# A list in place of a planner for the filler work between the last block's score steps

## The chip, the cores and the metric

The kernel runs on one core of one Trainium2 chip. The metric is the device time of one execution in microseconds (us), as the median of several runs. One execution was also taken by the hardware profiler; every duration below comes from that profile.

## What is computed

The input x has 2048 rows of 448 values (bfloat16). Its rows are normalised, and three terms are added:

```
xn  = layernorm(x)
A   = softmax(mask(q k^T / sqrt(28))) v @ wo      # 16 heads of 28; row i sees rows i-255 .. i
B   = (gelu(xn @ w_gate) * (xn @ w_up)) @ w_down  # inner width 1792
out = x + A + B
```

## The kernel before

**Tiling.** The rows are cut into four blocks of 512 (`NB` = 4, `QB` = 512). The inner width of 1792 is 14 slices of 128 (`NF` = 14); slices p and p+7 form a pair, since one weight load of 64 rows holds half of the inputs for each, so that the two matmuls of a pair run beside each other in the two halves of the array (`chunk`, L418; the matmul is L426). A pair takes seven chunks, 14 matmuls. The output of a block is four tiles of 128 rows; each tile (`gen_down`, L382) sums 4 matmuls with `wo` (L392, the attention's output `oN`) and 14 with `wd` (L397, the feed-forward's product `hT`) in one bank of PSUM, adds x on the vector engine (L402) and sends the rows out.

**Stages of a block.** Attention (L547) comes first, in ten steps. Each step has a group of score matmuls into the tile `sc` (L626), then one exponential of 128x2048 on ScalarE (L632), then three multiplications by masks on the vector engine (L534), which are queued only in the next step. `sc` takes four of the eight PSUM banks and there is one of it, so the scores of a step cannot start before the exponential of the step before is over. Three steps (4, 6 and 9, the dictionary `pvs`) begin with a PV product, which multiplies finished probabilities by v (L587) into two banks `ov`; the fourth product comes in the next stage. After a PV product ScalarE copies one half (L571) and the vector engine adds the other (L572). The sums of the softmax come from two 32x32 transposes on the vector engine (`sums` L559, `inverse` L567) with a reciprocal between (L560), and GpSimd scales the result into `oN` (`scale_o`, L553). The two transposes write the same single buffer (`l`), which the scaling reads.

Then comes the gated stage (`gated`, L448): for each of the seven pairs p a gate product into `gt` (L426), its gelu on ScalarE (L467), and a multiplication by the up product. Pairs in `early` have their up product already, copied to `hT` in SBUF by the vector engine (`gen_up`, L433, the copies are L444; the multiplication is L472). For other pairs the up product is made in this stage (`up`, L453), stays in PSUM as `u`, and is multiplied from there (L475). After each pair a hook does the next of `sums` and `inverse` with `scale_o` (`after`, L669).

**What sets the order.** The whole program is recorded in the order in which the Python code issues it; each engine runs its own instructions in that order and waits on semaphores. Filler matmuls are put between the score steps by generators, wrapped in a `Feed` (L34). `Feed.run` issues matmuls up to the next `yield`, which tells their planned nanoseconds; a negative number marks the end of a unit, and HOLD keeps a feed from going on within a step. The planner `share` (L55) runs feeds until a step's planned share is used up. In blocks 0 to 2 the fillers are the products for the next block, and from block 1 on the down tiles of the block before. In the last block, `feeds[0]` is the down work of block 2 (4 tiles, 72 matmuls) and a second feed makes up pairs ahead, five of them (L797), in steps that a dictionary `plan` names (L799). After the last gated stage the four down tiles of block 3 stand alone (L843 to L845); its last tile is cut in two halves.

**Banks.** The four PSUM banks beside `sc` are handed out first in, first out by `take` (L250) and returned by `give` (L261): a down tile takes one, an up pair two, a PV product two. `give` is called when the reading instruction is recorded, so the next user of the bank waits for that instruction on the chip.

Of the kernel before, what the change touches and what calls it, by code (L numbers as in the profile page):

```python
# [15 lines left out]
S, D, H, Dh, F = 2048, 448, 16, 28, 1792  # L16
P = 128
NT = S // P
NF = F // P
# [5 lines left out]
HOLD = True  # L25
# [29 lines left out]
def share(feeds, first, second):  # L55

    want = [first, second]
    while True:
        can = [i for i, f in enumerate(feeds) if f.gens and want[i] > 190 and not f.held]
        if not can:  # L60
            return
        i = max(can, key=lambda i: (not feeds[i].closed, want[i]))
        for f in feeds:
            if f is not feeds[i]:
                f.closed = False
        want[i] -= feeds[i].run()
# [9 lines left out]
def kernel(  # L76
# [305 lines left out]
    def gen_down(qb):  # L382

        hT, oN = hTs[qb], oNs[qb]
        for tt in range(4):
            t = 4 * qb + tt
            cs = slice(tt * P, (tt + 1) * P)
            for lo, up in ((0, D),) if t < NT - 1 else ((0, D // 2), (D // 2, D)):
                w = up - lo
                po = take("po")  # L390
                for g in range(4):
                    nc.tensor.matmul(po[:, 0:w], lhsT=oN[:, g, cs], rhs=wo[:, g, lo:up], start=(g == 0), stop=False,  # L392
                                     skip_group_check=True)
                    if g % 2:
                        yield 380 * w // D
                for f in range(NF):
                    nc.tensor.matmul(po[:, 0:w], lhsT=hT[:, f, cs], rhs=wd[:, f, lo:up], start=False, stop=(f == NF - 1),  # L397
                                     skip_group_check=True)
                    if f % 2 and f < NF - 1:
                        yield 375 * w // D  # L400
                res = work.tile([P, D], bf16, name="res", bufs=2)
                nc.vector.tensor_tensor(out=res[:, 0:w], in0=po[:, 0:w], in1=x_sb[:, t, lo:up], op=ALU.add)  # L402
                give(po)
                nc.sync.dma_start(out=outv[:, t, lo:up], in_=res[:, 0:w])
                last_res[:] = [res]
                yield 375 * w // D

    def new_hT(qb):
        hT = blk.tile([P, NF, QB], bf16, name="hT", tag="hT")
# [23 lines left out]
    def gen_up(qb, ps):  # L433

        for p in ps:
            us = [take("ue") for _ in range(2)]
            for c in range(7):
                chunk(us, wu, p, qb, c)
                if c == 2:
                    yield 640  # L440
                if c == 5:
                    yield 640, HOLD
            for i in range(2):
                nc.vector.tensor_copy(out=hTs[qb][:, p + 7 * i, :], in_=us[i])  # L444
            give(*us)
            yield -320

    def gated(qb, early, last_v, flush, hook):  # L448

# [97 lines left out]
    def attention(qb, feeds, aux, plan):  # L547
# [55 lines left out]
        for i, (scores, ncol, edges) in enumerate(steps):  # L603
            while (qb, scores[-1][0]) not in done:
                feeds[0].run()
            for fd in feeds:
                if fd.held:
                    fd.run()
            if i in pvs:
                pv(pvs[i])  # L610
            while fresh:
                apply_masks(*fresh.pop(0))
            if not qb and i - 1 in pvs:
                sums()
                inverse()
            if qb and i - 1 in pvs:
                sums()
            if qb and i - 2 in pvs:
                inverse()
            ss = phase[0].pool.tile([P, 4, QB], f32, name="sc", tag="s")  # L620
            p_sb = work.tile([P, 4, QB], bf16, name="p_sb", bufs=5)
            for g, half, kt, q0, nq, col in scores:
                k0, nk = (64 * half, 64) if half is not None else (0, P)
                for j in range(4):
                    r = slice(32 * j, 32 * j + Dh)
                    nc.tensor.matmul(ss[k0:k0 + nk, j, col:col + nq], lhsT=kT[r, g, kt * P + k0:kt * P + k0 + nk],  # L626
                                     rhs=qT[r, g, qb * QB + q0:qb * QB + q0 + nq], start=True, stop=True,
                                     tile_position=(32 * j, k0), skip_group_check=True)
                parts.setdefault(g, []).append((half, kt, q0, nq, col, p_sb))
            if not qb and i == 2:  # L630
                rstd(6, 2)
            nc.scalar.activation(out=p_sb[:, :, 0:ncol], in_=ss[:, :, 0:ncol], func=ACT.Exp, scale=SCALE)  # L632
            flush()
            if qb:
                fresh.append((p_sb, edges))
            else:
                for m in edges:
                    masked(p_sb, *m)
            while later:
                scale_o(*later.pop(0))  # L640
            left = len(steps) - i
            if left == 1:
                drain(feeds)
            elif not qb:
                share(feeds + [Feed()], 1e12, 0)
            else:
                to = plan.get(i, 0)
                whole = sum(f.left for f in feeds) + STEP * left + PV * sum(j > i for j in pvs)
                ahead = STEP + PV * (i + 1 in pvs) + (360 if to > 1000 else 0)
                late = 400 if i == 0 else 0  # L650
                want = (whole - late) / (left + 0.2) + late - ahead - to
                if i in pvs:
                    had = feeds[0].left
                    share(feeds[:1], min(1100, want), 0)
                    want -= had - feeds[0].left
                if qb == NB - 1:
                    share(feeds[:1], want, 0)
                    share(feeds, 0, to)
                else:
                    share(feeds, want, to)  # L660
            if aux:
                aux.pop(0)()

# [108 lines left out]
    for qb in range(NB):  # L772
        if qb in (1, 3):
            tc.mark_branch_hint_location("general", hint="LikelyTaken",
                                         engines=[mybir.EngineType.DVE if qb == 1 else mybir.EngineType.PE])
        early = ()
        aux, plan = [], {}
        if qb < 2:
            if qb:
                aux = [lambda: rstd(12, 4)]  # L780
            else:
                aux = [ahead, ahead2, ahead3, lambda: fill_pads(False), lambda: fill_pads(True), lambda: None,
                       lambda: stat(8), lambda: stat(9), lambda: stat(10), lambda: stat(11), lambda: rstd(8, 4)]
        if qb == 0:
            new_hT(0)
            early = (1, 2, 3)
            feeds = [Feed((gen_qk(0, (1, 2, 3), [(t, pvs[t]) for t in (2, 3)]), 3 * QK1 + 360),
                          (gen_up(0, (1,)), UP1), (gen_v(1, (4,)), 1500), (gen_up(0, (2,)), UP1), (gen_v(1, (6,)), 1500),
                          (gen_up(0, (3,)), UP1), (gen_qk(1, range(4)), PROJ - 3000))]
        else:  # L790
            feeds = [Feed((gen_down(qb - 1), DOWN))]
            if qb < 3:
                feeds.append(Feed((gen_proj(qb + 1), PROJ)))
                plan = {0: 1140, 1: 1140, 2: 1300, 4: 1300, 6: 1300, 7: 870}
            else:
                new_hT(3)
                early = (1, 2, 3, 4, 5)  # L797
                feeds.append(Feed((gen_up(3, early), UP1 * len(early))))
                plan = {1: 1280, 2: 1280, 4: 1280, 6: 1280, 7: 1280}  # L799
        if qb:  # L800
            swap(qb, nc.sync)
        score_pool(1)
        rest, after, flush = attention(qb, feeds, aux, plan)
        nc.scalar.preload_act_table(ACT.Gelu_apprx_tanh)
        score_pool(2)
        if qb not in hTs:
            new_hT(qb)

        def hook(f):
            after(f)  # L810
            if qb < 3 and f == 4:
                collect(qb + 1)
            if qb < 3 and f == 10:
                deliver(qb + 1)
            if f >= 4 and qb < 2:
                t = 4 * qb + 4 + f // 2
                if f < 12:
                    norm(t + 2)
                    dma_transp(t + 2)
                    if qb == 0:  # L820
                        stat(t + 6)

        gated(qb, early, rest, flush, hook)
        if qb < NB - 1:
            nc.scalar.preload_act_table_set("natural_log_exp_and_others")
# [142 lines left out]
```

## Time and profile before

| what | us |
|---|---|
| median of 3 runs | 219.06 (218.66 to 219.39) |
| the profiled execution's own time | 219.12 |
| its span in the trace | 217.40 |
| its time outside the span | 1.72 |
| TensorE (PE) busy in the span | 212.0 |
| vector engine (DVE) busy | 151.9 |
| ScalarE (ACT) busy | 132.8 |
| GpSimd (POOL) busy | 46.9 |
| block 3, first score matmul | starts at 157.02 |
| block 3, gated stage, first up pair | starts at 185.39 |
| last down tiles, first matmul | starts at 199.87 |

An instruction's row tells its start, its duration, its engine, the line of the code, and what it writes and reads. Matmuls overlap in their pipeline: a matmul of 448 columns shows 352 ns, but the next starts 189 ns after it. What a matmul costs the engine is therefore the distance from its start to the next one's start, not its duration. On the vector engine, too, the next instruction starts about 80 ns before the end of the one ahead where it does not depend on it.

### The profile page before, as it was taken

Reading aid. Unit: us, or ns where it says so; the run is one execution under the profiler, and the core shown is the slowest. Engines: PE = TensorE matmul, PEld = TensorE weight load, DVE = VectorE, ACT = ScalarE, POOL = GpSimd, SP = SyncE. Lnnn points to the kernel's source line nnn. Section 1 sums busy time; section 2 is a strip of 40 time slices with the busy share of each in tenths; the row PEclk is TensorE's granted clock in tenths of the full one; section 3 lists DMA queues with packets and bytes.
Section 4 is the critical chain, followed back from the end, with each engine's and each line's share of the span. In section 5 each row is a group of like instructions: output and inputs, shape, how many; then the busy total and the mean of one; then the engine's idle time right before and its main releaser. Section 6 shows DMA issues by size and latency. Waiting matters only on the chain.

```text
span 217.4 us, 6061 instructions
## 1 busy us (share of the span) xinstructions
PE 212.0 (97%) x2581; PEld 97.5 (45%) x2581; DVE 151.9 (70%) x346; ACT 132.8 (61%) x129; POOL 46.9 (22%) x80
## 2 busy tenths in 40 slices
PE   7999999999999999999999999999999999999993
PEld 2433343444444454444444544444444445444562
DVE  7787898599666883588566795477347799479521
ACT  4588779672978776613778788423576776565000
POOL 5277987320000130022000022022000022022001
PEclk9999999999999999999999999999999999999999
DMA  6993599933510000102320000200030000000011
GB/s 192 273 227 52 125 237 227 281 123 72 79 41 24 24 23 27 22 0 53 81 64 21 24 3 21 59 11 0 0 78 18 5 24 24 24 2 0 26 33 38
DMA packets 23232, 14.45 MB, mean 66 GB/s; under 512 B 9792, under 2 KB 23200, under 8 KB 23200
## 3 DMA queue, kind: packets, MB, share of 16 engines
q1 hardware_dynamic: 22256, 13.73, 26.9%
q8 instruction: 21, 0.34, 0.7%
q10 hardware_dynamic: 944, 0.29, 0.6%
q14 instruction: 11, 0.09, 0.2%
HBM read 8.69 MB, written 2.18 MB: 50 GB/s over the span
## 4 chain that ended last, share of the span: by engine, by line
PE 96%; ACT 1%; DVE 1%; issue 1%; DVEq 0%
PE po L397 21%; PE gt L426 20%; PE u L426 14%; PE sc L626 6%; PE po L392 6%; PE ue L426 6%; PE ov L587 5%; PE pq L237 4%; PE pv L237 4%; PE pk L237 3%; PE wps L196 2%; PE pq L243 1%; PE pv L243 1%; PE s L237 1%; ACT p_sb L632 0%
## 5 line engine op out<-in xcount | busy, mean ns | idle before, releaser
L632 ACT ACTIVATE p_sb<-sc 128x2048 bf16<-128x2048 f32 (+2 forms) x42 | 73.8, 1757 | 12.7 <-PE sc L626 9.4
L467 ACT ACTIVATE ge<-gt 128x1024 bf16<-128x1024 f32 x28 | 28.7, 1024 | 39.6 <-PE gt L426 39.0
L397 PE MATMUL po<-wd,hT 128*128 128x448 bf16 (+1 forms) x238 | 49.0, 342 | 0.0
L553 POOL TENSOR_TENSOR oN<-oc,l 128x512 bf16<-128x512 f32 x12 | 16.0, 1333 | 136.3 <-DVE l L567 85.3
L426 PE MATMUL gt<-xnT,wg 64*128 64x512 bf16 x224 | 45.3, 376 | 0.0
L426 PE MATMUL gt<-xsw,wg 64*128 64x512 bf16 x168 | 40.7, 376 | 0.0
L475 DVE TENSOR_TENSOR hT<-ge,u 128x512 bf16<-128x512 bf16 x40 | 25.8, 679 | 18.3 <-PE u L426 9.8
L426 PE MATMUL u<-xnT,wu 64*128 64x512 bf16 x160 | 33.2, 376 | 0.0
L397 PEld LDWEIGHTS <-hT 128*128 128x128 bf16 x238 | 21.4, 98 | 18.7 <-issue 2.8
L426 PEld LDWEIGHTS <-wu 64*128 64x128 bf16 x392 | 18.8, 94 | 23.8 <-issue 3.8
L426 PE MATMUL u<-xsw,wu 64*128 64x512 bf16 x120 | 29.1, 376 | 0.0
L426 PEld LDWEIGHTS <-wg 64*128 64x128 bf16 x392 | 18.8, 94 | 22.7 <-issue 0.3
L534 DVE TENSOR_TENSOR p_sb<-p_sb,masks 128x256 bf16<-128x256 bf16 (+1 forms) x90 | 26.8, 352 | 1.8 <-ACT p_sb L632 1.8
L626 PE MATMUL sc<-qT,kT 28*64 28x320 bf16 (+7 forms) x640 | 16.9, 263 | 0.2
L402 DVE TENSOR_TENSOR res<-po,x_sb 128x448 bf16<-128x448 f32 (+1 forms) x17 | 10.0, 589 | 8.8 <-PE po L397 8.6
L392 PE MATMUL po<-wo,oN 128*128 128x448 bf16 (+1 forms) x68 | 15.6, 343 | 0.0
L572 DVE TENSOR_TENSOR oc<-oc,ov 128x512 f32<-128x512 f32 x12 | 8.2, 686 | 10.6 <-ACT oc L571 10.6
L544 POOL TENSOR_SCALAR_AFFINE_SELECT p_sb<-p_sb 128x512 bf16<-128x512 bf16 (+1 forms) x20 | 14.2, 730 | 3.7 <-ACT p_sb L632 3.5
L426 PE MATMUL ue<-xnT,wu 64*128 64x512 bf16 x64 | 13.6, 377 | 0.0
L626 PEld LDWEIGHTS <-kT 28*64 28x64 bf16 (+1 forms) x640 | 7.8, 102 | 11.5 <-issue 9.9
L444 DVE CAST hT<-ue 128x512 bf16<-128x512 f32 x16 | 10.2, 678 | 3.8 <-PE ue L426 3.7
L559 DVE STREAM_TRANSPOSE l<-oc 128x512 f32<-128x512 f32 x16 | 11.2, 703 | 1.6 <-POOL oN L553 1.6
(89 smaller groups left out, 232.8 us busy)
## 6 DMA issues: line engine op xcount, KB each, us to landing
out_dram<-res SPq DMA_DIRECT2D x15, 112.0 KB
xsw<-xnT SPq DMA_DIRECT2D x8, 192.0 KB
x_sb<-in_A_x_dram SPq DMA_DIRECT2D x3, 448.0 KB
wu<-in_B_w_up_dram SPq DMA_DIRECT2D x4, 336.0 KB
wd<-in_B_w_down_dram SPq DMA_DIRECT2D x3, 448.0 KB
wg<-in_B_w_gate_dram SPq DMA_DIRECT2D x2, 448.0 KB
wg<-in_B_w_gate_dram SPq DMA_DIRECT2D x2, 336.0 KB
wraw<-in_A_wqkv_dram SPq DMA_DIRECT2D x2, 252.0 KB
```

Of the source, the lines that this page charges most:

```text
L237: nc.tensor.matmul(ps, lhsT=lhs(c), rhs=rhs(c), start=start and c == 0, stop=stop and c == 2, skip_group_check=True)
L392: nc.tensor.matmul(po[:, 0:w], lhsT=oN[:, g, cs], rhs=wo[:, g, lo:up], start=(g == 0), stop=False, skip_group_check=True)
L397: nc.tensor.matmul(po[:, 0:w], lhsT=hT[:, f, cs], rhs=wd[:, f, lo:up], start=False, stop=(f == NF - 1), skip_group_check=True)
L426: nc.tensor.matmul(ps, lhsT=w[r, c, p * P:(p + 1) * P], rhs=x, start=c == 0, stop=c == 6, tile_position=(64 * hi, 0), skip_group_check=True)
L467: nc.scalar.activation(out=ges[p][:, :, :], in_=gt[:, :, :], func=ACT.Gelu_apprx_tanh)
L475: nc.vector.tensor_tensor(out=hT[:, p + 7 * i, :], in0=ge[:, i, :], in1=u, op=ALU.mult)
L534: nc.vector.tensor_tensor(out=reg, in0=reg, in1=m, op=ALU.mult)
L544: nc.gpsimd.affine_select(out=reg, in_=reg, pattern=mid + [[1 if diag else -1, min(w, P)]], compare_op=ALU.is_ge, fill=0.0, base=0 if diag ...
L553: nc.gpsimd.tensor_tensor(out=oN[:, g, :], in0=oc[:, :], in1=inv, op=ALU.mult)
L559: nc.vector.transpose(out=l1[:, :, :].rearrange("p a b -> p (a b)"), in_=oc[:, :])
L626: nc.tensor.matmul(ss[k0:k0 + nk, j, col:col + nq], lhsT=kT[r, g, kt * P + k0:kt * P + k0 + nk], rhs=qT[r, g, qb * QB + q0:qb * QB + q0 + ...
L632: nc.scalar.activation(out=p_sb[:, :, 0:ncol], in_=ss[:, :, 0:ncol], func=ACT.Exp, scale=SCALE)
```

## The change

Four things change in the code.

1. `gen_down` yields after every matmul instead of every second one, and takes the 14 slices of `hT` in another order, with 6 and 13 last.
2. `gen_up` yields after each chunk; HOLD stays for block 0 alone.
3. In the last block, a list tells for each of the ten steps how many yields of the down feed `d` and of the up feed `u` are run, in place of the planner and `plan`. One yield of `d` is one matmul, one yield of `u` is a chunk, two matmuls that run beside each other.
4. `early` in the last block has six pairs, 1 to 6, not five.

```diff
     def gen_down(qb):
+        order = [f for f in range(NF) if f % 7 < 6] + [6, 13]
...
-                    if g % 2:
-                        yield 380 * w // D
-                for f in range(NF):
-                    nc.tensor.matmul(po[:, 0:w], lhsT=hT[:, f, cs], rhs=wd[:, f, lo:up], start=False, stop=(f == NF - 1),
+                    yield 187 * w // D
+                for n, f in enumerate(order):
+                    nc.tensor.matmul(po[:, 0:w], lhsT=hT[:, f, cs], rhs=wd[:, f, lo:up], start=False, stop=(n == NF - 1),
                                      skip_group_check=True)
-                    if f % 2 and f < NF - 1:
-                        yield 375 * w // D
+                    if n < NF - 1:
+                        yield 187 * w // D
...
-                yield 375 * w // D
+                yield 187 * w // D
...
     def gen_up(qb, ps):
                 chunk(us, wu, p, qb, c)
-                if c == 2:
-                    yield 640
-                if c == 5:
-                    yield 640, HOLD
+                if c < 6:
+                    yield (213, HOLD) if qb == 0 and c == 5 else 213
...
-            yield -320
+            yield 330
...
     def attention(qb, feeds, aux, plan):
             left = len(steps) - i
-            if left == 1:
+            if isinstance(plan, list):
+                for feed, n in plan[i]:
+                    for _ in range(n):
+                        feed.run()
+            elif left == 1:
                 drain(feeds)
...
-                if qb == NB - 1:
-                    share(feeds[:1], want, 0)
-                    share(feeds, 0, to)
-                else:
-                    share(feeds, want, to)
+                share(feeds, want, to)
...
                 new_hT(3)
-                early = (1, 2, 3, 4, 5)
-                feeds.append(Feed((gen_up(3, early), UP1 * len(early))))
-                plan = {1: 1280, 2: 1280, 4: 1280, 6: 1280, 7: 1280}
+                early = (1, 2, 3, 4, 5, 6)
+                d, u = feeds[0], Feed((gen_up(3, early), UP1 * len(early)))
+                feeds.append(u)
+                plan = [[(d, 11)], [(d, 7), (u, 3)], [(u, 11)], [(u, 7)], [(d, 18)], [(u, 7)], [(d, 13)], [(d, 5), (u, 6)],
+                        [(u, 8)], [(d, 18)]]
```

## The prediction, made before the changed kernel ran

> **What bounds the kernel now.** I read the page's first part, then its chain that ended last, then the same chain in order of time for block 3, then the timeline of the places that the change touches.
>
> ```profile
> PE 212.0 (97%) x2581; PEld 97.5 (45%) x2581; DVE 151.9 (70%) x346; ACT 132.8 (61%) x129; POOL 46.9 (22%) x80
> ...
> PE 96%; ACT 1%; DVE 1%; issue 1%; DVEq 0%
> ```
>
> The matrix engine is on the chain for 96% of the span. But a busy PE may hide a wait, so I compared distances from start to start. The chain in order of time (start, length, what) has them:
>
> ```profile
> 152.56 1.51 PE u L426 x14
> ...
> 161.42 1.62 PE ue L426 x14
> 163.04 0.35 PE sc L626 x16
> ...
> 185.46 1.62 PE u L426 x14
> 187.07 1.51 PE gt L426 x14
> ```
>
> The reader is to see two lengths for the same 14 matmuls: 1.51 when another up or gate product follows, 1.62 where a stretch is entered from, or left for, another shape (up is 64 rows deep, down 128, scores 32). In unrounded starts a matmul of 448 columns is followed after 189 ns by its like and after 282 to 285 by an up, PV or score matmul; an up pair after 213 by its like and after 306 by scores. **A switch of shape costs 93 to 96 ns.** From 157.02 to the end, each distance is its usual value or that plus a switch: before, the engine waits for nothing in block 3. Hence time can be won only by fewer switches, and is lost by every wait that the new order opens.
>
> **1. Fewer switches: -0.28 us.** Listed in issue order, block 3's score phase had 5 switches down to up, 5 up to scores, 3 down to PV, 1 down to scores: 14. Afterwards it has 2 down to up, 3 up to scores, 3 up to PV, 3 down to scores: 11. Leaving the scores costs the same whatever follows (block 0: 211 ns into up, 210 and 211 into q, behind the same 256 columns). The step from the last gate to the down tiles stays one switch. So 3 x 0.095 = 0.28. The sixth pair is 14 matmuls moved from the end of the gated stage into the score phase: no matmul is added. Its two vector multiplications from PSUM (680 ns each, L475) become two copies (680, L444) and one multiplication (650, L472).
>
> **2. Step 0 becomes too short: +0.37 us.** The table load delays its exponential:
>
> ```profile
> 156.71 1.28 ACT L825 ACT_TABLE_LOAD   x1
> ...
> 157.02 0.42 PE L626 MATMUL sc<-qT,kT 28*64 28x320 bf16 x16
> ...
> 158.01 1.88 ACT L632 ACTIVATE p_sb<-sc 128x2048 bf16<-128x2048 f32 x1
> ...
> 160.13 0.43 PE L626 MATMUL sc<-qT,kT 28*64 28x320 bf16 x24
> ```
>
> The exponential ends at 159.88; 14 down matmuls covered that, and the next scores started at 160.13. The list puts 11 there: 3 x 0.189 = 0.57 less, so PE is ready at 159.56. In block 0, where scores do wait, they start 0.05 behind the exponential (14.96 to 15.01): here 159.94. The wait is 0.37.
>
> The other steps: scores need 0.50 to 0.73 until the exponential starts, 1.88, and 0.05. Step 1 has 0.36 (scores) + 1.42 (7 down and a switch) + 0.74 (3 chunks and a switch) = 2.52 against 0.55 + 1.88 + 0.05 = 2.48. Steps 3 and 5 have 0.36 + 1.59 + 0.68 (PV) = 2.63 against 2.48. The rest are longer: 2.8 to 3.9. No wait, with 0.04 to spare in step 1.
>
> **3. The PV product of step 9 comes before its banks are free: +0.9 us.** Two up pairs now lie close together ahead of it (the sixth chunk of pair 5 in step 7, then pair 5's end and pair 6 in step 8), and the PV product takes pair 5's two banks, which the vector engine must first copy out (L444). That engine's queue ahead of these copies is, from the scores of step 6 on (call their start 0; in the profile 173.94): the addition of PV, masks of step 5, `inverse` of group 0, masks of step 6, `sums` of group 1, an output addition, masks of step 7, `inverse` of group 1.
>
> ```profile
> 176.15 0.70 DVE L567 STREAM_TRANSPOSE l<-inv_all 128x512 f32<-128x512 f32 x1
> ...
> 176.89 1.29 DVE L444 CAST hT<-ue 128x512 bf16<-128x512 f32 x2
> 177.02 1.27 POOL L553 TENSOR_TENSOR oN<-oc,l 128x512 bf16<-128x512 f32 x1 [25.64 <-PE ue L426]
> ...
> 182.46 1.27 POOL L553 TENSOR_TENSOR oN<-oc,l 128x512 bf16<-128x512 f32 x1 [4.17 <-DVE l L567]
> ...
> 182.81 1.60 DVE L534 TENSOR_TENSOR p_sb<-p_sb,masks 128x256 bf16<-128x256 bf16 x3
> ```
>
> Up to `inverse` the order is the old one, so it ends at 176.85, or 2.91. GpSimd's scaling, which started 0.17 behind it here and 0.08 behind it at the three later groups, then runs to 4.26 or 4.35. Before, two copies from PSUM filled that time, unharmed (1.29). Now the masks of step 6 stand there. Three masks take 0.82 alone, but 1.60 where they met a scaling (last pair of rows): they end some 0.6 behind it. With the usual overlap `sums` starts at about 4.65; it could not before the scaling's end in any case, since it overwrites `l`. Then by rows: `sums` 0.91, output addition 0.56, masks 0.74, `inverse` 0.62 to the next start: the first copy starts at 7.48 and ends at 8.17, the second at 8.77. PE's way: step 6 is 0.36 + 2.55 (13 down and a switch) = 2.91; step 7 0.36 + 1.04 (5 down) + 1.37 (6 chunks) = 2.77; step 8's 0.36 + 1.80 (8 chunks) brings it to 7.84. The first half of PV waits until 8.2, the second, which starts 0.003 behind it when nothing waits, until 8.8; of the 0.68 for PV only some 0.1 is done by then. **Wait: about 0.9.** Without the collision it is 0.6. If instead the mask starts first and holds GpSimd back, `sums` comes later and it is 1.1.
>
> The Trainium skill ("SBUF — State Buffer", section "Who interferes with whom") says that a vector operation with two SBUF inputs and a GpSimd operation that reads SBUF exclude each other, and that issue order decides who blocks. The trace agrees on the exclusion (1.60 against 0.82). By that rule the second mask, due at 3.03 by this reckoning, would go first if the scaling starts at 3.08, and the whole sum would be 0.2 higher. I keep GpSimd first, since three of four rows put its start 0.08 behind `inverse`, at 2.99.
>
> **4. The last down tiles reach `oN` too early: +0.47 us.** The sixth pair's 1.51 were the cover for GpSimd's last scaling:
>
> ```profile
> 197.67 1.62 POOL L553 TENSOR_TENSOR oN<-oc,l 128x512 bf16<-128x512 f32 x1 [2.27 <-DVE l L567]
> ...
> 199.87 0.93 PE L392 MATMUL po<-wo,oN 128*128 128x448 bf16 x4
> ```
>
> The scaling of group 3 ends at 199.29. It hangs on ScalarE's first gelu by a chain (transposes, multiplications, two scalings of 1.62) which the change leaves as it is; so it still ends 12.38 behind the start of the first gate product (186.91). PE now needs 1.60 for that gate, 0.67 for PV, 9.08 for the six other gates, 0.10 for the switch, and reaches the fourth `wo` matmul, which reads group 3, 0.57 later: at 12.02. Add 0.1 to 12.38 for signal and weight load: a wait of 0.47 (0.35 to 0.6). The new order of slices does its part: pair 6's product is ready some 1.4 before its matmul, and nothing else is late.
>
> **5. Finer yields in blocks 1 and 2: nothing.** In issue order, a few steps there give one down matmul (0.19) to a neighbour. The shortened steps had 0.40 and 0.56 between exponential and scores, and need 0.05. Down next to v products is no switch (189).
>
> **Sum.** -0.28 + 0.37 + 0.9 + 0.47 = +1.46 on the profiled execution's 219.12: 220.6. The median is 219.06, 0.06 lower, which is nothing here. Measurement can tell about 0.3%, 0.66 us, from no change.
>
> **The rivals.**
>
> - *As forecast*, within 219.9 to 221.0: 0.66.
> - *More waits*: steps 1, 3 and 5 have 0.04 to 0.15 to spare; a copy that delays a bank, or a recut step in blocks 1 and 2, adds 0.1 at each, +0.4 in all: 221.0 and somewhat over. Against it, step 1 alone is really close. 0.12.
> - *Only one of parts 3 and 4 binds.* PV's copies keep up, because the vector engine has idle times of 0.7 to 1.0 in this phase before: -0.28 + 0.37 + 0.47 = +0.56, 219.7. Against: those idle times lay where it waited for up products, and in steps 6 to 8 the list leaves none. 0.11.
> - *Not slower*: the vector engine's queue and the scalings run early enough for both PV and the down tiles. Then -0.28 + 0.37 = +0.09: 219.2. It decides from 0.9 us of the 5.8 us queue in part 3, and 0.47 in part 4. For it, pairs 3 and 4 are copied earlier than before; against it, each duration is a row. 0.07.
> - *Faster*: the scores at 160.13, 173.94, 176.78 and 182.27 each start 0.22 to 0.25 behind an exponential. If that were a wait in disguise, longer steps would free 4 x 0.2 = 0.8, and with half of parts 3 and 4 gone the time would be 218.3. Against: the distances there equal those of steps with 0.4 to spare, and block 0 restarts at 0.05. 0.04.
>
> That the list does not do what it says is excluded by the order of the built instructions: it gives 72 down yields and 42 chunks, as needed.
>
> **The numbers.** Likeliest 220.6. The range 219.6 to 221.3 leaves out the last two cases and tails of the others. Slower by over 0.3% (above 219.7): forecast, more waits and a part of the third, 0.82. Within: 0.14. Faster: 0.04.
>
> **What would show it.** In the changed profile: scores of step 1 at 0.05 behind the end of the first exponential; 0.9 lost between up and PV ahead of step 9's scores, behind copies L444; a scaling on GpSimd that masks of step 6 run into; 0.4 to 0.5 inside the first four `wo` matmuls, ended by L553. The forecast falls if PV starts right behind the up pair in step 9.

## The result and the profile after

| what | us |
|---|---|
| before, median of 6 runs | 218.99 (218.57 to 219.39) |
| changed, median of 6 runs | 220.13 (219.84 to 220.53) |
| changed over before | 1.0052 (1.0039 to 1.0064) |
| profiled execution of the changed kernel, its own time and its span | 220.07 and 218.2 |

The changed kernel is slower by half a per cent. The spans of the two profiled executions (217.4 and 218.2) differ by 0.8, which is less than what block 3 lost, since the changed kernel's execution happened to start block 1 earlier by 0.38 (54.87 against 55.24; see the last section). From block 1's first score to block 3's first score both take 101.78. I therefore compare one distance, from **block 3's first score to the last matmul**: 56.43 before, 57.63 after, **+1.20**. It is used for all runs below.

The page's part on the chain, of the changed kernel, answers to the 96% of before:

```profile
PE 84%; DVE 8%; ACT 3%; issue 2%; POOL 1%; DVEq 0%; ACTq 0%
```

PE is no longer nearly the whole chain. At a wait the chain passes to the engine waited for and follows that one back for as long as it is busy, so the missing 12% are not lost time: the waits, read below, add up to 1.52 us, 0.7% of the span. The waits of the changed kernel in block 3 and behind name them (engine and line, what it waited for: total us, times, longest):

```profile
PEld L393 <- POOL oN L551: 0.7, 1, 0.7
...
PE sc L624 <- ACT p_sb L630: 0.3, 1, 0.3
PE ov L585 <- DVE hT L442: 0.3, 1, 0.3
PE po L393 <- POOL oN L551: 0.2, 1, 0.2
```

Before, this list had no PE row. The idle times here count from the modelled end of a matmul, so they understate what was lost; distances from start to start give it. Line numbers are those of each run's own file: in the changed kernel `wo` is L393, and what comes after `gen_up` has moved up by two lines.

**Step 0.** The timeline of the changed kernel, from step 0's scores to step 1's:

```profile
156.65 0.42 PE L624 MATMUL sc<-qT,kT 28*64 28x320 bf16 x16
...
157.63 1.88 ACT L630 ACTIVATE p_sb<-sc 128x2048 bf16<-128x2048 f32 x1
157.77 1.49 PE L397 MATMUL po<-wd,hT 128*128 128x448 bf16 x7
...
159.56 0.43 PE L624 MATMUL sc<-qT,kT 28*64 28x320 bf16 x24 [0.31 <-ACT p_sb L630]
```

The exponential ends at 159.51 and the scores start 0.05 later. The distance from the last down matmul to the scores is 658 ns where a switch makes it 283: **0.375 lost**.

**Steps 6 to 9.** The vector engine's queue, GpSimd and the PV product, from the same timeline:

```profile
176.31 0.70 DVE L565 STREAM_TRANSPOSE l<-inv_all 128x512 f32<-128x512 f32 x1
176.94 1.86 DVE L532 TENSOR_TENSOR p_sb<-p_sb,masks 128x256 bf16<-128x256 bf16 x3
...
177.19 1.46 POOL L551 TENSOR_TENSOR oN<-oc,l 128x512 bf16<-128x512 f32 x1 [26.18 <-DVE l L565]
...
178.73 0.70 DVE L557 STREAM_TRANSPOSE l<-oc 128x512 f32<-128x512 f32 x1
...
181.47 2.44 DVE L442 CAST hT<-ue 128x512 bf16<-128x512 f32 x4
...
182.17 0.32 PE L585 MATMUL ov<-p_sb,v_sb 64*32 64x320 bf16 x4
182.77 0.73 PE L585 MATMUL ov<-p_sb,v_sb 64*32 64x320 bf16 x44 [0.28 <-DVE hT L442]
```

The three masks of step 6 take 1.86 instead of 0.82, since the third is locked out until GpSimd's scaling is over at 178.65: it alone shows 1.36 instead of 0.28, and ends 0.15 behind the scaling. The copies of pair 5 then start at 181.47, and PV begins in two parts, each some 0.05 behind the end of one copy (182.12 and 182.72). Distances of 455 instead of 306, and 587 instead of 3: **0.73 lost**.

**The last tiles.**

```profile
199.59 1.62 POOL L551 TENSOR_TENSOR oN<-oc,l 128x512 bf16<-128x512 f32 x1 [2.27 <-DVE l L565]
...
200.27 0.74 PE L393 MATMUL po<-wo,oN 128*128 128x448 bf16 x3
...
201.27 0.36 PE L393 MATMUL po<-wo,oN 128*128 128x448 bf16 x1 [0.25 <-POOL oN L551]
```

Three `wo` matmuls run, and the fourth waits for the scaling of group 3, which ends at 201.21: a distance of 603 instead of 189, **0.41 lost**.

The three add to 1.52; the distance grew by 1.20; so 0.32 was won elsewhere. Three switches fewer were expected to give 0.28; where the other 0.04 comes from is told with the last experiment.

### The profile page after: what moved, and what is told of

Same layout as the page of the kernel before. It is cut to its first block, busy times and chain, and to the rows that moved or that the text cites. A ratio compares the mean times of both kernels' runs of the same rounds, so it can differ in the third digit from the quotient of the medians.

```text
span 218.2 us, 6052 instructions
## 1 busy us (share of the span) xinstructions
PE 211.5 (97%) x2572; PEld 97.9 (45%) x2581; DVE 151.8 (70%) x347; ACT 132.8 (61%) x129; POOL 47.1 (22%) x80
## 4 chain that ended last, share of the span: by engine, by line
PE 84%; DVE 8%; ACT 3%; issue 2%; POOL 1%; DVEq 0%; ACTq 0%
PE po L397 18%; PE gt L426 15%; PE u L426 13%; PE sc L624 5%; PE po L393 5%; PE ue L426 5%; PE pv L237 4%; PE pq L237 4%; PE ov L585 4%; PE pk L237 3%; PE wps L196 2%; DVE p_sb L532 2%; POOL oN L551 1%; PE pq L243 1%; ACT p_sb L630 1%
## 5 line engine op out<-in xcount | busy, mean ns | idle before, releaser
L473 DVE TENSOR_TENSOR hT<-ge,u 128x512 bf16<-128x512 bf16 x38 | 24.5, 679 | 18.4 <-PE u L426 9.6
L426 PE MATMUL u<-xnT,wu 64*128 64x512 bf16 x152 | 31.5, 376 | 0.0
L397 PEld LDWEIGHTS <-hT 128*128 128x128 bf16 x238 | 22.4, 98 | 19.0 <-issue 1.8
L426 PE MATMUL u<-xsw,wu 64*128 64x512 bf16 x114 | 27.6, 376 | 0.0
L393 PE MATMUL po<-wo,oN 128*128 128x448 bf16 (+1 forms) x68 | 16.2, 343 | 0.2 <-POOL oN L551 0.2
L426 PE MATMUL ue<-xnT,wu 64*128 64x512 bf16 x72 | 15.3, 377 | 0.0
L426 PE MATMUL ue<-xsw,wu 64*128 64x512 bf16 x54 | 13.2, 377 | 0.0
L442 DVE CAST hT<-ue 128x512 bf16<-128x512 f32 x18 | 11.4, 676 | 2.1 <-PE ue L426 2.1
```

Of the source, the lines that this page charges most:

```text
L426: nc.tensor.matmul(ps, lhsT=w[r, c, p * P:(p + 1) * P], rhs=x, start=c == 0, stop=c == 6, tile_position=(64 * hi, 0), skip_group_check=True)
L473: nc.vector.tensor_tensor(out=hT[:, p + 7 * i, :], in0=ge[:, i, :], in1=u, op=ALU.mult)
```

## The experiments

Each run was timed in five rounds beside the kernel before. "Distance" is from block 3's first score to the last matmul.

| run | distance | time, median | over before (95% interval) |
|---|---|---|---|
| before | 56.43 | 218.99 to 219.06 | |
| changed | 57.63 | 220.13 | 1.0052 (1.0039 to 1.0064) |
| e1_step0 | 57.28 | 219.58 | 1.0035 (1.0024 to 1.0046) |
| e2_wo_late | 57.21 | 219.90 | 1.0040 (1.0025 to 1.0055) |
| e2b_wo_after12 | 57.80 | 220.40 | 1.0064 (1.0046 to 1.0082) |
| e3_chunk | 57.26 | 219.67 | 1.0035 (1.0023 to 1.0046) |
| e9_no_scaling | 57.03 | 219.61 | 1.0028 (1.0013 to 1.0042) |
| e5_yields_only | 56.82 | 219.65 | 1.0023 (1.0011 to 1.0035) |
| e4_three | 56.48 | 219.18 | 1.0001 (0.9988 to 1.0013) |
| e7_copies_first | 56.13 | 218.81 | 0.9988 (0.9974 to 1.0002) |
| e8_switches | 56.98 | 219.61 | 1.0028 (1.0015 to 1.0041) |

Against the kernel before, the medians move as the distances do, within 0.3 us. The intervals of the five runs with a single edit of the changed kernel (e1 to e3 and e9) all overlap that of the changed kernel, so by time alone they can hardly be told from it: what they show is read from their traces, one execution each.

### Step 0: e1_step0

```diff
-                plan = [[(d, 11)], [(d, 7), (u, 3)], [(u, 11)], ...
+                plan = [[(d, 13)], [(d, 5), (u, 5)], [(u, 9)], ...
```

> The changed kernel with the first three entries of the list recut: 13 down in step 0, 5 down and 5 chunks in step 1, 9 chunks in step 2. Theory (the exponential of step 0, held up by the table load, is what step 1's scores wait for): that wait of 0.38 us goes, steps 1 and 2 are then 2.56 and 2.37 us long against 2.48 and 2.42 needed, so 0.05 comes back: 0.3 less than the changed kernel, some 219.8 us, with the waits at step 9's PV and at the fourth wo matmul as they were. Rival (time lost in step 0 is only moved, since the first steps have too little work in all): 0.1 or more waits again in front of the scores of steps 2 or 3, and the time stays at 220.1.

Measured: the wait is gone, 57.28, 0.36 less; 0.02 is left ahead of step 3's scores (a distance of 326 instead of 306). The waits at PV and at the fourth `wo` are as before (454 and 589, 600). The timeline of this run has no wait in front of step 1's scores:

```profile
157.41 1.88 ACT L630 ACTIVATE p_sb<-sc 128x2048 bf16<-128x2048 f32 x1
157.55 1.86 PE L397 MATMUL po<-wd,hT 128*128 128x448 bf16 x9
...
159.34 0.43 PE L624 MATMUL sc<-qT,kT 28*64 28x320 bf16 x24
```

So the first steps had enough work in all; it was in the wrong ones.

### The last tiles: e2_wo_late and e2b_wo_after12

```diff
-                for g in range(4):
-                    nc.tensor.matmul(... oN[:, g, cs] ... start=(g == 0) ...)
-                for n, f in enumerate(order):
-                    nc.tensor.matmul(... hT[:, f, cs] ... stop=(n == NF - 1) ...)
+                heads = [(oN, wo, g) for g in range(4)]
+                ffs = [(hT, wd, f) for f in order]
+                seq = heads + ffs if qb < NB - 1 or tt else FIRST
```

`FIRST` is the order of the first tile of block 3: the ten slices of pairs 0 to 4, `heads`, then slices 5, 12, 6 and 13 in the first run; `ffs[:12] + heads + ffs[12:]` in the second.

> The changed kernel, where the first down tile of block 3 takes its matmuls in another order: ten slices of hT (pairs 0 to 4), then the four with wo, then the slices of pairs 5 and 6. Theory (the wait of 0.41 us in the last tiles is for GpSimd's scaling of group 3): the wait goes, since the fourth wo comes 1.9 us later; 219.7 us. Rival (the vector engine's products for pairs 5 and 6 are just as late, and oN only hides them): a wait of 0.4 us stays, at one of the last four matmuls of that tile, and the time stays at 220.1.

> As the run with late wo, but twelve slices (pairs 0 to 5) come before wo. In the changed kernel's trace the product of pair 5 is locked out by GpSimd's scaling and ends 0.5 us behind it, and its matmul would now stand sixth, 0.95 us behind the tile's start. Theory (scaling and lock together set what is ready when): the wait is not removed but grows to about 0.6, in front of the sixth matmul, behind the vector engine's L470; 220.3 us. Rival (only oN is late): no wait, 219.7 us.

Measured: with ten slices ahead the wait is gone and the distance falls by 0.42. With twelve ahead it is 0.17 longer than in the changed kernel: the sixth matmul comes 778 ns behind the fifth, a wait of 0.59. The timeline of that run shows why:

```profile
199.78 1.62 POOL L550 TENSOR_TENSOR oN<-oc,l 128x512 bf16<-128x512 f32 x1 [2.27 <-DVE l L564]
200.23 2.32 DVE L469 TENSOR_TENSOR hT<-ge,hT 128x1024 bf16<-128x1024 bf16 x2
...
200.46 1.12 PE L396 MATMUL po<-wd,hT 128*128 128x448 bf16 x5
...
202.01 1.31 PE L396 MATMUL po<-wd,hT 128*128 128x448 bf16 x6 [0.42 <-DVE hT L469]
```

Five matmuls run; the sixth reads the product of pair 5, which was locked out by the scaling until 201.40 and ended 0.55 later. Both `oN` and that product are late because of the same scaling; the order of ten, four, four steps around both.

### PV of step 9: e3_chunk and e9_no_scaling

```diff
-                [(d, 5), (u, 6)], [(u, 8)], [(d, 18)]]
+                [(d, 5), (u, 7)], [(u, 7)], [(d, 18)]]
```

> The changed kernel with one chunk moved from step 8 to step 7, so that pair 5 ends in step 7 (5 down, 7 chunks; then 7 chunks). Its copies out of PSUM are then queued ahead of step 7's masks and of the transpose of group 1. Theory (step 9's PV product waits for pair 5's two banks): the wait of 0.74 us in front of and inside PV goes. The copies of pair 6 are still queued behind masks and transpose, and step 9's down tile takes one of its banks, so 0.35 to 0.5 comes back in front of that tile's first wo: 0.25 to 0.4 less than the changed kernel, 219.8 us. Rival (PV waits for the masks of step 7 on its probabilities): those masks come 1.2 us later than before, and the wait in front of PV grows; 220.5 us or more.

Measured: 0.38 less. The wait around PV is gone, and one of 0.36 (499 instead of 137) has come in front of the first `wo` of step 9's down tile:

```profile
181.75 0.82 DVE L532 TENSOR_TENSOR p_sb<-p_sb,masks 128x256 bf16<-128x256 bf16 x3
...
182.41 0.75 PE L585 MATMUL ov<-p_sb,v_sb 64*32 64x320 bf16 x48
...
183.11 1.25 DVE L442 CAST hT<-ue 128x512 bf16<-128x512 f32 x2
...
183.81 0.92 PE L393 MATMUL po<-wo,oN 128*128 128x448 bf16 x4 [0.29 <-DVE hT L442]
```

The masks of step 7 now end 0.16 behind PV's start, and PV does not wait: it was the banks, not the probabilities. The second run takes GpSimd's scaling out of this place:

```diff
         def scale_o(g, oc, inv):
+            if qb == NB - 1 and g == 0:
+                nc.scalar.copy(out=oN[:, g, :], in_=oc[:, :])
+                return
```

> The changed kernel, but in the last block group 0 is not scaled on GpSimd: ScalarE copies it unscaled (so the output leaves out the softmax's division for heads 0 to 3 of block 3). Nothing else is moved. Theory (step 9's PV wait of 0.74 us exists because GpSimd's scaling and the masks of step 6 lock each other out, 1.86 us for masks that take 0.82 alone): the vector engine's queue is 1.0 us earlier, and the wait falls to 0.15 or less: 57.63 - 0.6 = 57.0 us from block 3's first score to the last matmul, 219.5 us. Rival (the list simply gives the vector engine too much in steps 6 to 8, with or without the lock): 0.5 or more of the wait stays, 57.4 us, 220.0.

Measured: 57.03, 0.60 less, as the theory had it. The masks of step 6 take 0.79, and `sums` (L560) follows at once:

```profile
176.88 0.79 DVE L532 TENSOR_TENSOR p_sb<-p_sb,masks 128x256 bf16<-128x256 bf16 x3
...
177.59 0.71 DVE L560 STREAM_TRANSPOSE l<-oc 128x512 f32<-128x512 f32 x1
...
181.97 0.88 PE L588 MATMUL ov<-p_sb,v_sb 64*32 64x320 bf16 x48
```

`sums` starts 1.33 behind the start of step 6's transpose, where it was 2.41. The masks of step 7 then wait for their exponential, so the copies are 0.6 earlier, and of the 0.73 at PV 0.14 is left, between its halves. So four fifths of that wait come from the scaling, and the rest from the queue as it is. That the lock, by which scaling and masks exclude each other, is the cause, as the theory says, is not shown: without the scaling, `sums` need not wait for the buffer `l` either, and in the changed kernel scaling and third mask ended within 0.15 of each other. An estimate from rows says that the buffer alone would do most of it. Without the lock the scaling would take 1.27 and end at 177.19 + 1.27 = 178.46, and in the kernel before a transpose that waited for `l` started 0.04 behind a scaling (195.43 behind 195.39): `sums` would start at 178.50, 0.23 earlier than it did, of the 1.08 by which it is late. A second buffer `l` was not tried.

### The finer yields alone: e5_yields_only

The kernel before with the changed `gen_down`, and nothing else.

> The kernel before, with gen_down alone as changed (a yield after each matmul, slices 6 and 13 last); planner, plan and five early pairs as before. Theory for blocks 1 and 2 (moving single down matmuls between steps costs nothing): block 3's first score starts as far behind block 1's first score as before, 101.78 us. In the last block the planner cuts other steps: it leaves the last down matmul of a tile to step 2, right ahead of an up pair that takes this tile's bank, whose output addition is queued behind the masks: a wait of about 0.4 there, 219.4 us. Rival (the yields do nothing anywhere): 219.0 us and no wait.

Measured: 101.78 from block 1's to block 3's first score, and a wait of 0.41 in front of the second half of an up pair in step 2 (417 instead of some 3):

```profile
162.89 1.29 DVE L444 CAST hT<-ue 128x512 bf16<-128x512 f32 x2 [2.14 <-PE ue L426]
...
163.81 0.39 PE L426 MATMUL ue<-xnT,wu 64*128 64x512 bf16 x1
...
164.23 0.39 PE L426 MATMUL ue<-xsw,wu 64*128 64x512 bf16 x2
...
164.83 0.61 DVE L402 TENSOR_TENSOR res<-po,x_sb 128x448 bf16<-128x448 f32 x1
```

The size is as expected, but the cause is another. The wait ends 0.05 behind the second copy of the up pair before (163.50 to 164.18), and the output addition, which the expectation blamed, starts only 0.60 after the wait is over. Since the tile now ends in step 2, its bank is returned behind both banks of that pair, and the queue of banks hands the new pair those two. In the kernel before, the tile's bank came first, and the new pair took it and the pair's first. In blocks 1 and 2 the yields cost nothing; in the last block they would have cost 0.4 under the planner. The list ends its tile in step 1, and the changed kernel shows no such wait.

### Together: e4_three, e7_copies_first, e8_switches

> The three single edits that removed a wait, together (first three list entries recut, late wo in the first down tile of block 3, one chunk from step 8 to step 7). Theory (the waits are independent, since PE waits for nothing between them): from the changed kernel's 57.63 us between block 3's first score and the last matmul, 0.36, 0.42 and 0.38 go as in the single runs: 56.47; the wait of 0.5 at step 9's first wo stays. Time as before, 219.0. Rival (each removed wait is partly given back to the next): 56.7 or more, 219.3.

Measured: 56.48, as the sum of the single gains has it. The waits are independent. One remains, 0.36 at step 9's first `wo`. The next run moves the vector engine's transpose, in step 8, behind the copies:

```diff
-            if qb and i - 2 in pvs:
+            if qb and i - 2 in pvs and not (isinstance(plan, list) and i == 8):
                 inverse()
...
                 for feed, n in plan[i]:
                     for _ in range(n):
                         feed.run()
+                if i == 8:
+                    inverse()
+                    scale_o(*later.pop(0))
```

> The three edits together, and in step 8 of the last block the transpose of group 1 and its scaling are issued behind the copies of pair 6 instead of ahead of pair 5's. Theory (that transpose, 0.63 us, is what makes pair 6's copies late for step 9's down tile): the wait of 0.5 goes, no wait over 0.05 is left in block 3, and what remains against the kernel before are three switches of shape fewer: 56.43 - 0.28 + 0.05 = 56.2 us from block 3's first score to the last matmul, 218.8 us, 0.1% under the kernel before. Rival (the scaling, now later, is in some other way late): a wait in front of PV of group 3 or of the last tiles, and 56.5 or more.

Measured: 56.13, 0.30 under the kernel before, with no wait over 0.02. By time it is 218.81 and the ratio 0.9988, with an interval that just reaches 1: a gain that the trace shows and the timing hardly tells. The last run adds eight switches to it:

```diff
-                [(d, 5), (u, 7)]
+                [(d, 1), (u, 1), (d, 1), (u, 1), (d, 1), (u, 1), (d, 1), (u, 1), (d, 1), (u, 3)]
```

> As the run with copies first, but step 7's 5 down matmuls and 7 chunks alternate: one down, one chunk, four times, then one down and three chunks. The same work with eight more switches of shape. Theory (a switch costs 93 to 96 ns wherever it stands): 0.75 us more than the run with copies first, 56.95 us and 219.5. Rival (a switch costs only where a stretch of its own length ends, or its cost overlaps when stretches are a single matmul): 0.2 or less more, 219.0.

Measured: 0.85 more, 0.106 a switch. The chain of this run in order of time shows one down matmul and one chunk in turn (start, length):

```profile
177.07 0.30 PE po L396
177.36 0.32 PE ue L425 x2
177.69 0.29 PE po L396
```

A down matmul costs 295 instead of 189, a chunk 318 instead of 214. The cost does not vanish in short stretches. It is 0.01 above the 93 to 96 ns because these count only the distance across the switch, and the first distance behind a switch is longer too. In block 3 of the kernel before, the first down matmul of each of 11 stretches is followed after 199 or 200 ns, every other one after 189 or 190; the first up or gate pair of each of 7 stretches after 222 to 224, every other one after 212 or 213. With these 10 ns a switch costs 0.103 to 0.106, which gives the 0.85 here and the 0.32 of three switches.

## Why the prediction was right

Measured +1.14 by the medians against +1.46 forecast; 220.13 lies in the range, and its side was right. The mechanisms were the four that were named; three sizes were off by little.

1. **Switches**, forecast -0.28: the traces leave -0.32, and e7 with a wait of 0.02 is at -0.30. The price of 0.095 left out the 10 ns of the first distance behind a switch; the 1.51 and 1.62 that the prediction shows for the same 14 matmuls already differ by 0.11.
2. **Step 0**, forecast +0.37: 0.375. The 0.05 behind the exponential, read in block 0, held in block 3.
3. **PV of step 9**, forecast +0.9: 0.73, the term that was most mis-sized. The first copy was reckoned to end at 8.17 behind step 6's scores (174.11) and ended at 8.02: the masks followed the output addition after 0.48, not 0.56, and the copy took 0.65, not 0.69. PE came at 7.92, not 7.84. Who goes first was wrong too: the scaling started 0.17 behind the transpose, as in the one row that I had set aside, so the second mask went first. That gave GpSimd the wait (1.46 instead of 1.27) and left one mask behind it instead of two, and `sums` started at 4.62, where 4.65 was forecast. That this agrees is in part luck: the row that the forecast used has the masks end 0.68 behind the scaling (184.41 against 183.73), and taken as it stands it gives 4.26 + 0.68 - 0.08 = 4.86. The Trainium skill's rule ("SBUF — State Buffer", section "Who interferes with whom": issue order decides who blocks) was right about the order; the 0.2 that I put on it did not come, since the work behind the lock shrank as the lock moved back.
4. **Fourth wo**, forecast +0.47: 0.41. The scaling ended 12.39 behind the first gate's start, as reckoned (12.38); signal and weight load took 0.06, not 0.1.
5. **Blocks 1 and 2**, forecast 0: 0, by the traces and by e5.

Of the rivals, "more waits" and "only one binds" did not come: step 1 had 0.07 to spare. "Faster", by waits in disguise at 0.22 to 0.25, falls, since released scores of block 3 start at 0.05. Its 218.3 does not come out of its own terms either: 219.12 - 0.28 + 0.37 + 0.69 (half of parts 3 and 4) - 0.8 is 219.1.

The gain of the idea, fewer switches, was there. It was a third of a microsecond, and the list spent nearly five times as much by leaving three releases uncovered.

## What to carry to other kernels

When one engine is on the chain throughout, a new order of its work wins only what it removes of that engine's own time; price that first, and then look up, for each stretch that becomes shorter or moves earlier, whose release it used to cover. A queue of another engine that looks idle on average can still be late at one point: add up its order from the last release on, and put whatever frees a buffer ahead of whatever only feeds a later stage.

## What was not expected of the hardware

The profiled executions reach block 1's first score between 54.65 and 55.34, whatever was changed behind it. Much of this goes back to the point at which the matmuls at the start begin to run twice as fast. Ten warm-up matmuls come first and follow each other at 427 ns; three short transposes come next. The same three in the kernel before, and then in the changed kernel:

```profile
5.61 0.53 PE L230 MATMUL tp<-ident,xn 128*128 128x128 bf16 x3
```

```profile
5.49 0.33 PE L230 MATMUL tp<-ident,xn 128*128 128x128 bf16 x3
```

From start to start they take 107 ns before, and 56 in the changed kernel; before, transposes follow at 56 only from 6.60 on. In e9 the warm-up matmuls themselves change from 427 to 216 after 3.91, and in e4 transposes still follow at 107 at 6.8. The profile's granted clock shows 1.00 in all of these slices, so only the distances tell it. The Trainium skill ("TensorE: Matmul & The Clock Gate", Part 1) says that the clock is released by a window that runs freely, so that the point varies from run to run; these traces agree that it varies, between some 4 and 7 us. The start of block 1 varies less, by 0.7 us, and not by this alone: e2b, with an early change (its ten took 3.45 from first to last, against 3.81 before), took 0.35 more from block 0's first score to block 1's than the kernel before, and why was not followed up. Half a per cent of this kernel is 1.1 us, so spans of single executions should not be compared without this stretch.
